# Making the second copy of a small weight on chip, in a fused attention and ReGLU kernel: one load instead of two, a matmul and two casts, the last tile's outputs in fresh buffers, and a new order of pieces

## The chip, the cores and the metric

The kernel runs on one core of one Trainium2 chip. The metric is the device time of an execution in microseconds (us), lower is better. Before the change, four runs gave 385.4, 385.94, 387.39 and 387.7 us; their median is 386.66. The engines are named as in the profile: PE (TensorE, matmul; PEld is its weight load), DVE (VectorE), ACT (ScalarE), POOL (GpSimd), SP (SyncE, which here only issues DMAs).

## What is computed

A linear attention with an exponential feature map, and a ReGLU feed-forward on its output. Shapes: q, k, v are 8 x 8 x 576 x 64 (batch, head, position, width), w_phi is 64 x 128, the feed-forward (FFN) has 4608 rows, width 512 and hidden width 1536; all in float32.

```python
def phi(x):
    proj = np.einsum('bhsd,df->bhsf', x, w_phi)
    proj = proj - np.max(np.abs(proj), axis=-1, keepdims=True)
    return np.concatenate([np.exp(proj), np.exp(-proj)], axis=-1)
q_p, k_p = (phi(q), phi(k))
kv = np.einsum('bhsf,bhsd->bhfd', k_p, v)
z = np.sum(k_p, axis=2)
num = np.einsum('bhsf,bhfd->bhsd', q_p, kv)
den = np.einsum('bhsf,bhf->bhs', q_p, z)[..., None] + 1e-06
x = num / den          # then rows (batch, position), columns (head, width)
gate = np.maximum(x @ w_gate, 0.0)
out = (gate * (x @ w_val)) @ w_out
```

## The kernel before

**Tiling.** Of the 576 positions of a batch, 512 are worked in four chunks of 128 rows; the last 64 ("tails") of two batches are put together into mixed tiles. Matmuls are bf16 with PSUM sums in float32. PSUM is one tile `pall` of eight banks of 512 float32 columns, and each piece of work is told by hand which banks it uses.

**Attention.** For each batch and each pair of heads (an item, u = 0 to 3) PE transposes k (L239; from batch 2 on a DMA does it), DVE copies the transpose to SBUF (L242), `rows_group` multiplies by w (L265) into a pair of banks, DVE takes the row maximum of the absolute values (L246), ACT makes exp of plus and minus the projection into `kp` (L279) and from the maximum the scales `ek` (L291, for batch 0 also a column of `vs`, L295), POOL scales v into `vs` (L250) and PE multiplies `kp` with `vs` into kv (L332, and L340 for the tail, whose scaled v is `vsm`); ACT copies kv (L348). For the first tail the scales are `ekm` (L302). For q, `q_rows` makes the projection twice, once as columns (L366, w as the weights) and once as rows for the maximum; ACT makes exp (L381 or L383/L384), PE multiplies with kv (`q_num`, L411: first 7 heads, then 1), DVE adds two terms into `u` (L420, L423) and takes the reciprocal `r` (L426), POOL divides into `xu` (L428), and `q_finish` transposes into `xT`: on PE with a DVE copy for batches 0 and 1 (L438, L444), by DMA on SP's queue after that (L434).

The projections contract over 64 rows only, so two heads lie in the two halves of the partitions, and w is needed in both halves: the tile `w2` is 128 x 128, w above w. It was made by two loads of w_phi into the two halves of `wf` on ACT's DMA queue (L1027) and one cast by ACT (L1037).

**FFN.** Nine groups: one for each batch's 512 rows and one for all the tails. In a group `half_step` makes twelve steps of x @ w_val (cast to `val_sb` by ACT, L475) and of x @ w_gate (DVE multiplies, L479) on PE (L466), and `out_step` multiplies with w_out in three parts (L492), after which ACT copies the tile to `out_sb` (L502) and SP stores it (L505; in the last group `store_pair`, L512, on SP's and ACT's queues). `out_last` (L519) makes the fourth tile of the last group in three column ranges of 256, 128 and 128, each copied by DVE (L528) and stored at once. `out_sb` has two buffers.

**What sets the order.** All of this is cut into 855 pieces, and the string `ORDER` says in which order the pieces are emitted, so it sets the order on every engine and queue at once. A token such as `44:0` is piece 44 with bank 0 (a pair starts at its first bank); `z22:0` is `keep_busy`, 22 units of 128 columns of a matmul on zeros (L1004) that computes nothing. Pieces 0 to 42 are the loads in the order of `LOADS`, 43 to 49 are the first item of batch 0 (transpose, projection, maximum with scales, two exps, vs, kv), 50, 57 and 64 begin the other three, 71 the first tail, 76 and 90 q of batch 0; 531 is the first FFN matmul. The first loads stand ahead of the list (L1022 to L1032).

The framework gives each DMA that SP or ACT issues one of eight completion lanes in turn; a DMA whose lane is still taken waits at the head of its queue for the DMA that held it. In the program's list of waits the second load of v's first tail (SP, L180) waits for the lane of the first V load.

Of the kernel before, what the change touches and what calls it, by code (L numbers as in the profile page):

```python
# [8 lines left out]
FP32 = mybir.dt.float32  # L9
BF16 = mybir.dt.bfloat16  # L10
# [36 lines left out]
ORDER = """z22:0 43:01 z1:2 50:2 44:0 0 z6:3 51:6 45 46 z5:5 64:5 47 57:4 71:3 48 z3:2 65:4 3 54 72:2 58:0 73  # L47
74 4 66 75 52 53 68 59 55 67 69 62 49:2 7 z16:3 76:3 60 56:6 8 1 61 2 90:7 77:42 91:60 78 79 9 70:2
5 93 63:3 108:4 103:5 120:0 83 94:13 92 6 95 96 z2:5 80:50 11 104:6 81:3 10 106 z20:4 100:45 84:02
101:5 85 82:4 105 12 114:5 531:4 86 102:0 532:1 87:76 115:4 109:2 126:0 117 537:1 547:6 110 13 17  # L50
88:7 111 538:0 97:16 553:7 545:0 107 116 539:6 121:2 127:0 112 129 122 546:7 16 14 123 89:4 132:5
540:6 98:7 533:4 145:5 549:6 128 554:7 176 124 133:24 118 135 130 534:6 134 15 550:7 136:04 137 138
113:2 99:3 125:6 174 548:7 555:5 119:6 146:30 131:2 148 19 543:7 139:62 551:0 140:1 541:7 142:26 147
542:0 158 177 143:1 535:7 552:6 168 195 544:2 149:03 169:6 556 20 150 151 170 171 141:2 557 21 144:3
155:40 536:1 558:2 559 189 190:3 560 191 18 152:01 561:7 159 175 183 193 153:2 564:6 156:5 565 192
160:02 161 201 196:4 162 227 566 562 197 198 154:2 157:3 163:01 563 164:62 22 214 571:3 199 172 229
583:1 567:0 184:2 178:4 186 179 568:1 579:0 180 185 584:7 573:6 200:1 580:0 202:24 181 204 247 23
203 182:7 589:6 194:1 572:0 187 25 205:42 248:6 26 206 188:1 575:0 207 249 241 574:2 228 250 576:3
211:45 587:0 173 235 208:12 577:3 212:0 569:7 242:5 230:2 295 232 243 244 590:4 24 570:7 209:1 297
578:0 585:4 581:7 231 215:50 217 586:4 588:7 210 216 582:2 218:03 236:5 245 251 213 219 29 237 597:7  # L60
233 591:2 598 220 239 224:01 238 225:3 592 221:41 279 599 310 252:0 226 253 222:3 593 240:5 266 223
254:60 256 246:4 296 304 234:5 289 255 280 594:3 33 335 165:2 257:04 258 259 30 595 600:2 166:7
290:4 291 596 27 263:67 292 601 602 167 298 264:7 260:30 261:1 603:6 28 615:7 617:0 316 294 267:24
311:6 313 293 269 268 604:1 312 262 607:0 616:4 31 348 618:5 605:1 606:6 305:2 270:40 265 271 609:7
623:6 272 306 356 608:0 308 307 624:1 276:45 273:07 625:6 613:1 626:5 614:2 36 281:36 317:0 282 35
314 611:5 322 619:2 400 283 318 32 621:6 277:7 620:3 284:24 612:5 319 274:3 309:7 315:6 610:4 299:0
320 323:25 278 301 325 275 622:7 350 627:4 362 324 285:56 628 34 629 300 630:7 302 326:25 357:0 42
327 328 636:4 358 631 321:5 632 401 416 351:2 352 637 349 360 353 633:5 634 635 37 639:6 354 303:7
638 647:2 286:3 359 329:56 368 640:7 655:4 330:6 332:23 657:5 287:7 418 649:4 658:6 331 336:02 363:4
361:7 643:6 338 364 39 644:7 425 437 650:2 656:3 38 648:6 333:7 334 337 365 641:2 651:3 339:06 369:4  # L70
340 341 659:2 645:3 370 355:6 342:70 374 660:1 652:2 646:3 402:60 371 419 438:4 469 366 403 404
642:2 367:3 653:0 372 431 439 343:1 405:26 373:7 440 654:3 345:70 661:1 346:6 662:2 672:5 673 344
410 432:3 375:06 434 441 376 663:2 347 674 433 377 664 665 435 669:3 378:04 411:6 379 387 670 412
666:2 380 667 384:01 381:45 413 417 414 668 671 382:1 675:0 385:2 471 687:7 388:53 420:0 390 421
691:2 422 676:7 692:3 679:4 689:7 693:2 389 40 690:3 680:4 383 688:7 288 677:0 391:13 392 386 393
426:5 697:7 427 698:0 41 521 443 415 442:3 394:41 428 694:2 423 397:73 483 683:0 398:1 681:4 395:2
695:5 424:6 678:0 696:7 484:5 444:31 429 436:0 446 445 485 477 682:7 685:0 430:1 684:2 699:7 486
686:3 705:4 478:5 447:02 480 700 449 448 706 489 470 479 456 399 396 707 708:2 701 453:35 709 450:46
711:7 702:5 451:3 454:6 710 703 457:03 704 717:2 459 481 458 712:7 723:6 718:5 719:7 460:30 461 487
472:5 508 462 725:2 473 726:7 731:0 466:13 732:4 729:2 724:7 452 463:01 730:4 475 522 464:7 467:3  # L80
455 713:2 474 715:1 714:0 495 727:4 716:7 490:5 496:20 498 720:4 497 465 468 721:7 491 744:0 492
738:1 406:74 722:2 728:3 733:4 734:2 488:3 745 407:7 482:6 746 735:2 493 499:35 494:7 500 741:0 501
476:7 739 740 502:34 742 505:15 743 753:6 506:7 736 737 503:3 747:4 509:05 749:7 510 748:2 754:3
767:4 755:7 511 751:3 504 752:2 512:04 514 750:3 756:2 523:64 513 768:3 759:2 525 760:0 757:1 515:23
516:0 758:4 518:51 765:3 524 766:2 763:0 780:1 519:3 764:4 761:5 769:0 507 762:2 770:7 777:0 526:65
774:7 517 778 771:2 520 527:34 775 528:5 776 779 772 785:3 408:0 787:4 795:5 529:3 781 782 773 783:0
784:1 786:7 796:0 788:6 791:7 793:5 789:6 803:7 792:0 790:1 804:2 797:0 805:1 813:7 798:0 794:6
810:5 801:4 799:6 800:3 814 802:4 409 806:6 811 530 816:0 812 815 807:6 819:1 808 817 831:7 809 818
823:7 820:1 827:0 828:2 825:1 824:0 821:7 826:6 841:5 822:7 832:6 829:0 833:7 839:1 840:0 830:2
842:1 835:0 836:7 834:6 837:5 846:7 838:6 843:0 847 848 852:1 853:2 854:3 844 849:7 845 850 851"""  # L90
# [6 lines left out]
def kernel(  # L97
# [56 lines left out]
    def psum_pair():  # L154
        i = plan.banks.pop(0)
        return pall[:, i : i + 2]
# [101 lines left out]

    def rows_group(halves, n=4):

        banks = psum_pair()
        for j in range(n):
            for i, (par, T4) in enumerate(halves):
                rows = slice(D * par, D * (par + 1))
                nc.tensor.matmul(  # L265
                    banks[:, i, F * j : F * (j + 1)], lhsT=T4[rows, j, :], rhs=w2[rows]
                )
        return banks[:, :, 0 : F * n].rearrange("p i (j f) -> p i j f", f=F)
# [188 lines left out]
    def ffn_pieces(g):  # L457
# [30 lines left out]
        def out_step(t, part):  # L488
            if part == 0:
                st["po", t] = psum()  # L490
            for fi in range(4 * part, 4 * part + 4):
                nc.tensor.matmul(  # L492
                    st["po", t],
                    lhsT=st["h2"][:, fi, P * t : P * t + P],
                    rhs=wo_sb[:, fi, :],
                    start=(fi == 0),
                    stop=(fi == NFC - 1),
                )
            if part < 2:
                return  # L500
            out_sb = sb_g.tile([P, DM], FP32, name="out_sb", bufs=2)
            nc.scalar.copy(out_sb, st["po", t])  # L502
            if g < B:
                rows = out[S * g : S * g + SF, :].rearrange("(p c) n -> c p n", c=C)
                nc.sync.dma_start(out=rows[t], in_=out_sb)  # L505
            else:
                store_pair(t, out_sb, 0, DM)

# [7 lines left out]
        def out_last(t, lo, hi):  # L516
            ps = psum()[:, 0 : hi - lo]
            for fi in range(NFC):
                nc.tensor.matmul(  # L519
                    ps,  # L520
                    lhsT=st["h2"][:, fi, P * t : P * t + P],
                    rhs=wo_sb[:, fi, lo:hi],
                    start=(fi == 0),
                    stop=(fi == NFC - 1),
                )
            if "last" not in st:
                st["last"] = sb_g.tile([P, DM], FP32, name="out_sb", bufs=2)
            nc.vector.tensor_copy(st["last"][:, lo:hi], ps)  # L528
            store_pair(t, st["last"], lo, hi)
# [8 lines left out]
        for n, (fis, lo, hi) in enumerate(steps):  # L538
            for name, w in (("wv", wv_sb), ("wg", wg_sb)):
# [13 lines left out]
                    (["h2"] if n == 0 else []) if gate else ["val"],  # L553
# [6 lines left out]
        for t in range(3 if g == B else 4):  # L560
            for part in range(3):
                ops = [("PE", NF * (0.0025 + DM / 2400))]
                if part == 2:
# [13 lines left out]
                    ["osb"] if part == 2 else [],  # L577
                    [("osb", 3), ("h2", 0, uses, g)] if part == 2 else [],
# [4 lines left out]
        if g == B:  # L583
            for i, (lo, hi) in enumerate(((0, 256), (256, 384), (384, 512))):
# [13 lines left out]
                    ["osb"] if i == 0 else [],  # L598
                    [("h2", 0, uses, g)] + ([("osb", 4)] if i == 2 else []),
                    [(g, "out", 3, i - 1)] if i else [],  # L600
# [386 lines left out]
    wf = singles.tile([P, F], FP32)  # L987
# [36 lines left out]
    )  # L1024
    for u in range(2):
        load_kqv(0, "kn", k, nc.sync, FP32, slice(2 * u, 2 * u + 2))
        nc.scalar.dma_start(out=wf[D * u : D * (u + 1)], in_=w_phi)  # L1027
# [5 lines left out]
    make_identity(nc, ident[FP32])  # L1033
    nc.gpsimd.tensor_copy(ident[BF16], ident[FP32])
    held = singles.tile([P, 1], FP32)
    nc.gpsimd.tensor_copy(held, inputs["kn", 0][:, 2, 0, 0:1])
    nc.scalar.copy(w2, wf)  # L1037
# [115 lines left out]
```

## Time and profile before

| | |
|---|---|
| median of 4 runs | 386.66 us (385.4 to 387.7) |
| the profiled execution's own time | 385.4 us |
| its span, first to last instruction | 383.6 us |
| idle PE up to the first FFN matmul at 31.08 | 8.7 us |
| after the last matmul (ends 379.1) to the end of the span | 4.5 us |

The page's section 2 cuts the span into 40 slices of 9.6 us; a digit is a busy share in tenths, PEclk the granted PE clock:

```profile
PE   7589999999999999999999999999999999999995
DVE  4479968767977788377957675487257643321430
ACT  3988857798868877759786967557555423224311
POOL 3776954476783565744267140623020201000000
PEclk9699999999999999999999999999999999999998
DMA  8979999989979998999157910301030112002004
```

PE is busy nearly throughout from the fourth slice on; the other engines thin out as the attention ends and only FFN is left. In the second slice the PE clock was low. A line of the timeline gives start, length, engine, line, operation, output and inputs, count, and in brackets the idle time just before with what ended it; the shares of the chain and the waits are inferred from semaphores, and the ends of matmuls are modelled.

### The profile page before, as it was taken

The numbers are of one execution on the slowest core, as the hardware profiler recorded it, in microseconds if no ns is written. First come the engines' busy times: TensorE is split into PE (matmuls) and PEld (weight loads), VectorE is DVE, ScalarE is ACT, GpSimd is POOL, SyncE is SP. The second block draws the span as 40 slices with busy tenths as digits, with TensorE's granted clock in tenths as the row PEclk, the third lists the DMA queues.
The fourth block names the chain that finished last, engine by engine and source line by source line (L and its number), as shares of the span: only waits on it lengthen the run. The fifth ranks groups of instructions, "written<-read, shape, count | busy, mean of one in ns | idle before, by whom it ended". The sixth has DMA issues, their size and how long they took to land.

```text
span 383.6 us, 8885 instructions
## 1 busy us (share of the span) xinstructions
PE 367.2 (96%) x3544; PEld 207.9 (54%) x3594; DVE 238.3 (62%) x410; ACT 242.3 (63%) x489; POOL 151.7 (40%) x166
## 2 busy tenths in 40 slices
PE   7589999999999999999999999999999999999995
PEld 4368988556465455555544555454644454444452
DVE  4479968767977788377957675487257643321430
ACT  3988857798868877759786967557555423224311
POOL 3776954476783565744267140623020201000000
PEclk9699999999999999999999999999999999999998
DMA  8979999989979998999157910301030112002004
GB/s 216 240 125 206 199 191 180 187 232 137 153 133 125 241 219 106 206 214 159 32 119 185 153 29 28 110 3 27 29 109 3 29 55 84 0 34 77 0 4 109
DMA packets 92282, 44.95 MB, mean 117 GB/s; under 512 B 58064, under 2 KB 87760, under 8 KB 92240
## 3 DMA queue, kind: packets, MB, share of 16 engines
q1 hardware_dynamic: 63328, 30.03, 35.9%
q0 software_dynamic: 28272, 13.77, 29.7%
q10 hardware_dynamic: 640, 0.59, 0.6%
q8 instruction: 28, 0.46, 0.5%
q14 instruction: 14, 0.11, 0.1%
HBM read 37.81 MB, written 9.44 MB: 123 GB/s over the span
## 4 chain that ended last, share of the span: by engine, by line
PE 92%; DMA 3%; issue 2%; ACT 1%; DVE 1%; SPq 0%; POOL 0%; DVEq 0%; POOLq 0%
PE pall L466 49%; PE pall L492 24%; PE pall L411 5%; PE pall L332 4%; PE pall L265 4%; PE pall L366 3%; DMA vt<-in_v_dram 2%; DMA vn<-in_v_dram 1%; PE pall L340 1%; PE pall L519 1%; PE pall L239 1%; ACT qp L383 1%; ACT qp L384 0%; PE pall L1004 0%; PE pall L438 0%
## 5 line engine op out<-in xcount | busy, mean ns | idle before, releaser
L479 DVE SCALAR_TENSOR_TENSOR h<-pall,val_sb 128x512 bf16<-128x512 f32 x108 | 74.0, 688 | 64.4 <-PE pall L466 60.9
L492 PE MATMUL pall<-wo_sb,h 128*128 128x512 bf16 x401 | 97.2, 379 | 1.3 <-issue 0.3
L475 ACT CAST val_sb<-pall 128x512 bf16<-128x512 f32 x108 | 63.0, 594 | 53.8 <-PE pall L466 48.7
L466 PE MATMUL pall<-xT,wv_sb 128*128 128x512 bf16 (+1 forms) x520 | 93.2, 320 | 0.6 <-DVE xT L444 0.2
L466 PE MATMUL pall<-xT,wg_sb 128*128 128x512 bf16 (+1 forms) x507 | 91.7, 319 | 1.1 <-issue 0.3
L428 POOL TENSOR_TENSOR xu<-u,r 128x512 bf16<-128x512 f32 x36 | 37.3, 1040 | 127.5 <-DVE r L426 104.6
L279 ACT ACTIVATE kp<-pall 128x1024 bf16<-128x1024 f32 (+1 forms) x74 | 70.4, 1009 | 5.1 <-PE pall L265 5.1
L250 POOL TENSOR_TENSOR vs<-vn,ek 128x1024 bf16<-128x1024 f32 x32 | 60.8, 1903 | 31.0 <-ACT ek L291 29.4
L466 PEld LDWEIGHTS <-wg_sb 128*128 128x128 bf16 x576 | 46.7, 98 | 39.9
L466 PEld LDWEIGHTS <-wv_sb 128*128 128x128 bf16 x576 | 46.4, 98 | 39.1 <-issue 0.3
L492 PEld LDWEIGHTS <-h 128*128 128x128 bf16 x420 | 38.4, 98 | 40.9
L246 DVE TENSOR_REDUCE mq<-pall 128x8 f32<-128x1024 f32 x36 | 43.9, 1221 | 13.3 <-PE pall L265 10.5
L246 DVE TENSOR_REDUCE mk<-pall 128x8 f32<-128x1024 f32 (+1 forms) x37 | 43.7, 1189 | 10.3 <-PE pall L265 5.2
L420 DVE TENSOR_TENSOR t<-pall,cq 128x455 f32<-128x455 f32 (+3 forms) x80 | 33.6, 420 | 26.3 <-PE pall L411 26.2
L502 ACT COPY out_sb<-pall 128x512 f32<-128x512 f32 x35 | 20.6, 589 | 37.3 <-PE pall L492 35.7
L383 ACT ACTIVATE qp<-pall 128x512 bf16<-128x512 f32 x60 | 36.6, 610 | 4.5 <-PE pall L366 4.3
L423 DVE TENSOR_TENSOR u<-pall,t 128x455 f32<-128x455 f32 (+3 forms) x80 | 34.2, 428 | 6.6
L384 ACT ACTIVATE qp<-pall 128x512 bf16<-128x512 f32 x60 | 37.1, 618 | 0.0
L411 PEld LDWEIGHTS <-qp 128*128 128x128 bf16 x640 | 28.2, 98 | 13.4 <-issue 0.4
L411 PE MATMUL pall<-kv,qp 128*128 128x65 bf16 x640 | 31.0, 194 | 0.3 <-ACT qp L384 0.2
L332 PE MATMUL pall<-vs,kp 128*128 128x65 bf16 x512 | 21.4, 196 | 3.1 <-ACT kp L279 2.2
L332 PEld LDWEIGHTS <-kp 128*128 128x128 bf16 x512 | 19.3, 99 | 7.6 <-ACT kp L279 2.4
(72 smaller groups left out, 260.6 us busy)
## 6 DMA issues: line engine op xcount, KB each, us to landing
out_dram<-out_sb SPq DMA_DIRECT2D x32, 256.0 KB, 2.4
vn<-in_v_dram SPq DMA_DIRECT2D x7, 1024.0 KB, 7.2
qn<-in_q_dram POOLq DMA_DIRECT2D x8, 512.0 KB, 8.2
kn<-in_k_dram POOLq DMA_DIRECT2D x7, 512.0 KB, 7.7
wv_sb<-in_moe_w_val_dram POOLq DMA_DIRECT2D x3, 512.0 KB, 10.3
wg_sb<-in_moe_w_gate_dram POOLq DMA_DIRECT2D x3, 512.0 KB, 13.9
wo_sb<-in_moe_w_out_dram POOLq DMA_DIRECT2D x3, 512.0 KB, 14.4
vt<-in_v_dram SPq DMA_DIRECT2D x6, 128.0 KB, 5.4
```

The costliest lines, as they stand in the source:

```text
L246: nc.vector.tensor_reduce(m, banks, axis=AX.X, op=ALU.max, apply_absolute_value=True)
L250: nc.gpsimd.tensor_tensor(dst[:, :, :, 0:D], src[:, :, None, :].to_broadcast([P, *dst.shape[1:3], D]), ek[:, :, :, None].to_broadcast([P, ...
L279: nc.scalar.activation(kp[:, s], st["rows"], AF.Exp, scale=(1.0, -1.0)[s])
L332: nc.tensor.matmul(kv_ps[:, hh, s, :], lhsT=st["kp"][:, s, c % 2, 2 * hh + c // 2], rhs=st["vs"][:, 4 * hh + c, s, :], start=(hh == s == c ...
L383: nc.scalar.activation(x["qp"][:, s, a], cols[:, 0], AF.Exp, scale=sign)
L384: nc.scalar.activation(y["qp"][:, s, b], cols[:, 1], AF.Exp, scale=sign)
L411: nc.tensor.matmul(banks[s][:, i], lhsT=x["qp"][:, s, slot, P * blk : P * (blk + 1)], rhs=kvs[b, h // 2][:, h % 2, s, :],)
L428: nc.gpsimd.tensor_tensor(x["xu"], x["u"][:, :, 0:D], r.to_broadcast([P, 8, D]), op=ALU.mult)
L466: nc.tensor.matmul(ps[:, n * i : n * (i + 1)], lhsT=w[:, dc, P * fi : P * fi + P], rhs=xT[:, dc, lo:hi], start=(dc == 0), stop=(dc == NDC ...
L475: nc.scalar.copy(st["val", step], ps)
L479: nc.vector.scalar_tensor_tensor(st["h2"][:, fis[0] : fis[-1] + 1, lo:hi], ps.rearrange("p (a b) -> p a b", b=n), 0.0, st["val", step].rea ...
L492: nc.tensor.matmul(st["po", t], lhsT=st["h2"][:, fi, P * t : P * t + P], rhs=wo_sb[:, fi, :], start=(fi == 0), stop=(fi == NFC - 1),)
```

## The change

- w_phi is loaded once, as 64 x 128, ahead of the k loads in program order, and cast by ACT to bf16 (`w1`). POOL writes `twice`, two 64 x 64 identities side by side, from the float32 identity, ahead of the bf16 identity. In front of the first projection PE multiplies `twice` with `w1`, which gives w above w in bank 7, and ACT copies it to `w2`.
- In the last group all four output tiles go into a tile that takes the room of `vn0` (a v buffer) instead of the two `out_sb` buffers, and the three column ranges of the fourth tile have to come after the other three tiles. Before, they stood ahead of the last two of them.
- `ORDER` is another list throughout, with other banks. There are 98 units of zeros instead of 77. The first wv load (piece 1) comes right after the loads of k and v of batch 1.
- With one DMA fewer the lanes shift by one: the second load of v's first tail waits for the second k load.

```diff
-ORDER = """z22:0 43:01 z1:2 50:2 44:0 0 z6:3 51:6 45 46 z5:5 64:5 47 57:4 71:3 48 z3:2 65:4 3 54 72:2 58:0 73
-74 4 66 75 52 53 68 59 55 67 69 62 49:2 7 z16:3 76:3 60 56:6 8 1 61 2 90:7 77:42 91:60 78 79 9 70:2
-5 93 63:3 108:4 103:5 120:0 83 94:13 92 6 95 96 z2:5 80:50 11 104:6 81:3 10 106 z20:4 100:45 84:02
...
-842:1 835:0 836:7 834:6 837:5 846:7 838:6 843:0 847 848 852:1 853:2 854:3 844 849:7 845 850 851"""
+ORDER = """z22:0 43:01 z6:2 44:6 45 50:5 0 46 z23:4 51:0 47 64:2 53 57:3 71:4 z5:5 58:2 3 72:6 60 73 61 48 4 52
+8 65:4 74 66 67 1 75 49:6 7 69 59 62 55 z11:7 76:7 90:6 9 68 z9:2 77:24 54 2 78 70:7 79 63:6 z4:0
+91:04 56:2 93 114:3 103:7 5 120:6 80:24 6 81:5 z7:3 104:6 83 92 z9:3 94:30 106 95 105 96 108:2 82:5
...
+839:7 842:5 833:6 849:7 834:0 840:1 843:2 838:0 844 850 845 846:3 851 847 848 852:4 853:5 854:6"""
...
+    w_ready = []
+
+    def both_halves_of_w():
+
+        ps = pall[:, 7, 0:F]
+        nc.tensor.matmul(ps, lhsT=twice.rearrange("p a b -> p (a b)"), rhs=w1)
+        nc.scalar.copy(w2, ps)
+        w_ready.append(True)
+
     def rows_group(halves, n=4):
 
+        if not w_ready:
+            both_halves_of_w()
         banks = psum_pair()
...
-            out_sb = sb_g.tile([P, DM], FP32, name="out_sb", bufs=2)
+            out_sb = sb_g.tile([P, DM], FP32, name="out_sb", bufs=2) if g < B else final(t)
             nc.scalar.copy(out_sb, st["po", t])
...
+        def final(t):
+
+            if "final" not in st:
+                st["final"] = sb_in.tile([P, H, C, D], FP32, name="vn0")
+            return st["final"].rearrange("p h c d -> p (h c d)")[:, DM * t : DM * (t + 1)]
...
-            if "last" not in st:
-                st["last"] = sb_g.tile([P, DM], FP32, name="out_sb", bufs=2)
-            nc.vector.tensor_copy(st["last"][:, lo:hi], ps)
-            store_pair(t, st["last"], lo, hi)
+            out_sb = final(t)
+            nc.vector.tensor_copy(out_sb[:, lo:hi], ps)
+            store_pair(t, out_sb, lo, hi)
...
-                    [(g, "out", 3, i - 1)] if i else [],
+                    [(g, "out", 3, i - 1)] if i else [(g, "out", t, 2) for t in range(3)],
...
-    wf = singles.tile([P, F], FP32)
+    wf = singles.tile([D, F], FP32)
+    w1 = singles.tile([D, F], BF16)
...
+    nc.scalar.dma_start(out=wf, in_=w_phi)
     for u in range(2):
         load_kqv(0, "kn", k, nc.sync, FP32, slice(2 * u, 2 * u + 2))
-        nc.scalar.dma_start(out=wf[D * u : D * (u + 1)], in_=w_phi)
...
     make_identity(nc, ident[FP32])
+    twice = singles.tile([D, 2, D], BF16)
+    nc.gpsimd.tensor_copy(twice, ident[FP32][0:D, None, 0:D].to_broadcast([D, 2, D]))
     nc.gpsimd.tensor_copy(ident[BF16], ident[FP32])
...
-    nc.scalar.copy(w2, wf)
+    nc.scalar.copy(w1, wf)
```

## The prediction

> **What bounds the kernel now.** I read the page's busy shares first, then the busy time by stretch, cut where the trace changes its character, then the chain of waits of the first 35 us, then the timeline there and at the end.
>
> ```profile
> PE 367.2 (96%) x3544; PEld 207.9 (54%) x3594; DVE 238.3 (62%) x410; ACT 242.3 (63%) x489; POOL 151.7 (40%) x166
> ```
> ```profile
> 0.00:31.08 31.08, 22.42 (x259) 14.82 (x260) 18.12 (x38) 22.50 (x53) 20.10 (x26) 0.89 0.99 195
> 31.08:371.90 340.82, 337.62 (x3231) 188.71 (x3280) 219.19 (x370) 218.01 (x434) 131.61 (x141) 1.00 0.65 111
> 371.90:379.10 7.20, 7.15 (x57) 4.37 (x55) 1.01 (x3) 1.17 (x2) 0.00 (x0) 1.00 0.28 73
> 379.10:383.70 4.60, 0.00 (x0) 0.00 (x0) 0.00 (x0) 0.58 (x1) 0.00 (x0) 0.72 0.43 116
> ```
> Columns: stretch, length, then busy us (count) of PE, weight load, DVE, ACT, POOL, then granted PE clock, DMA share, GB/s. From 31.08, the first FFN matmul, to 371.90 PE idles 3.2 us in 341: that stage is PE's own work, the new order can't take more than 3.2 us from it, and it can add. The two ends are open: 8.7 us idle in the first 31 (several us of the busy time there are matmuls on zeros that hold the clock up), and 4.6 us after the last matmul.
>
> The chain through the head, and the rows that set it:
> ```profile
> 1.76 5.64 DMA vn<-in_v_dram
> 7.42 6.22 DMA vt<-in_v_dram
> 13.85 1.81 issue
> 15.66 0.26 POOL vsm L257
> ```
> ```profile
> 6.44 0.30 ACT L1037 CAST w<-wf 128x128 bf16<-128x128 f32 x1 [4.21 <-DMA wf<-in_w_phi_dram]
> 6.79 0.40 PE L265 MATMUL pall<-w,tT 64*128 64x128 bf16 x8 [1.05 <-ACT w L1037]
> 7.23 1.22 DVE L246 TENSOR_REDUCE mk<-pall 128x8 f32<-128x1024 f32 x1 [0.76 <-PE pall L265]
> ```
> ```profile
> 12.50:19.30 6.80, 4.40 (x41) 3.19 (x42) 1.94 (x3) 6.02 (x19) 5.49 (x4) 0.50 1.26 261
> ```
> The second half of v's tail is only issued when an earlier V load has landed (7.4), and POOL waits for it until 13.81. Everything else in the head waits for w: the first projection stands 1.05 us for ACT's cast, and the cast for the second of w's two loads. And PE runs at half clock from 12.5 to 19.3.
>
> **The change part by part.** All sums are against this execution: span 383.6, time 385.4, so 1.8 us lie around it; it is 1.26 us below the median of 386.66.
>
> *One load of w instead of two.* Both loads stand on ACT's queue, not Pool's as the title has it; Pool gains a 64x128 copy. The tile's rows give 2.8 us to landing for the first (issued 0.97, so 3.8) and 4.7 for the second (1.6, so 6.3). The one that stays is first in its queue: 3.8. New on the path: w1's cast (0.30 by L1037, ready 4.2, hidden: PE is at its first transposes until about 4.7), 6 units of zeros (22 took 2.53 us at the start, so 0.7; to 5.4), the doubling matmul (between 0.05, the mean of eight in the row above, and 0.31, the lone 128-wide one at 4.57; I take 0.1, since it follows other matmuls), and the copy to w2 from PSUM (between 0.30, the cast above, and 0.40, a 128x260 copy of L348; 0.3, being the size of the cast). With 0.1 of hand-offs the projection starts at 5.9, not 6.79: **0.9 us earlier**. Without an early landing (6.3) it would start at about 7.2, 0.4 later than now. Behind ACT's wait for PE stand only exponentials that need w2 anyway. Pool's extra copy (at most 0.29, its cast of 128x128) lies in Pool's 1.31 us wait before `held`: nothing; uncovered 0.3 on the transposes that need `ident`.
>
> *A lane moves.* The listed waits of SP show that with one DMA fewer the second v-tail load waits for the second K load (issued 1.26, 3.1 to landing, so 4.4), not for the V load that lands at 7.4. It issues at 5.6 and, right behind the first half (5.0 plus 6.9), lands about 12.1 instead of 13.64. A bound from below is no gain, if it is the DMA rate (busy share above 1 until 19) that sets it; from above 1.8, the earlier issue. I take 1.5: it joins a queue whose previous piece is down at 11.9.
>
> *The head in the new order*, laid out from the instruction lists with the durations of this trace (now in brackets). DVE's maximum ends 7.55, so ACT's `ek` starts 7.6 [8.48]. ACT then has `ek`,`vs` 0.42, four exponentials of 0.94 and `ekm` 0.8: `ekm` is ready at 12.6 [12.5], since one more exponential stands before it. So `vsm` starts 12.6 [13.81] and the last matmuls of the first kv at 14.9 [15.96]. Then 11 + 9 units of zeros, 16 transposes and two 512-wide matmuls, at half clock 0.107 per 128 columns as zeros cost there: 4.7, so the first q projection is there at 19.6 and its exponentials start [20.96]. Pool's three `vs` (1.9 each) end at 20.6 [21.4], the last kv is copied at 22.8, the first numerators run at 23.2 [25.39]. DVE has two maxima and three casts before them, so `t` at 24.35 [26.41], `r` at 26.25, `xu` at 26.3 [28.48]; a tail maximum, a q maximum and a cast now stand ahead of xT's copy: 28.6 [30.64]. The first FFN matmul at 29.25 [31.08]: **1.8 us earlier**. The list of pieces ahead of it is the same in both orders, so PE has no more real work left after it. The zeros grow from 77 to 98 units: 1.1 us at full clock, all ahead of that matmul and inside this layout, so not counted again. At full clock throughout the same layout ends 0.8 earlier.
>
> Here a rule speaks against the change. The trace shows half clock for 6.8 us after PE had stood from about 10 to 13.5 with one 0.40 us group in it. In the new order PE stands from about 11.3 (16 kv matmuls that need only the first `vs`) to 14.9. The Trainium skill (TensorE: Matmul & The Clock Gate, "HAM oscillation — how this bites in real kernels") says that a gap above some 3.4 us puts PE back to half rate, at windows that run freely. By the row, half clock until 19.3 as now: 1.8 us gained. By the rule, a gap of 3.6 that starts later can bring a later window, half rate until about 26: PE has some 4 us (at full rate) of work there, that doubles, about 2 us of it has room beside ACT and DVE, so the gain is gone. I take the row: the gap is no longer than the present one and zeros fill more of what lies ahead of it.
>
> *Loads moved.* Pool issues the first wv load at about 10.7 instead of 21.39, into a time in which the DMA engines go idle later on (share 0.04 at 20 to 22), and the other four from 20.6, 0.5 earlier, with one load less ahead. Now they land about 2.6 us apart from 27.2 on; each should come about 3 us earlier, and PE wants them 1.8 earlier: hidden. Pool's 0.8 of issuing ends before `vsm`: nothing.
>
> *Tail.* PE's work is the same. Now the last tile ends in an ACT copy of 0.58 and 64 KB stores (2.0 and 2.3 us to landing); then in DVE's 128-wide copy of 0.29 and a quarter of the bytes (1.9 and 2.1 for 32 KB). So **0.45 us earlier** (0.3 to 0.7). The fresh output buffer takes away waits that the trace doesn't show on the path: the copies there wait for PE. Nothing.
>
> *The order from 31 to 372.* Every engine's list is another one. Between at best 3.2 us less and a loss that one late transfer sets; I take no change, as the stretches now idle by 0.1 to 0.7 us in every 30 to 70, and the supply starts earlier too.
>
> Sum: 1.8 + 0.45 = 2.3, 383.1 for the profiled execution, **384.4** for the median.
>
> **The rivals.**
> *Head gain absorbed*: half clock lasts on into 19 to 26, or the first FFN matmuls meet late weights. For it: the rule, and a DMA share of 1.2 to 1.5 from 24 to 60. Against it: PE waited for no weights there, 28.87 busy of 28.92. Only the tail stays: 386.2.
> *A stall in the middle (the other side)*: SP's queue is strict in order, and the new order sets other stores and V loads ahead of the transposes that make xT. SP's own waits now show 62.5 us in 13 on `xu`, 4.8 each, none reaching PE. One such wait laid bare on PE costs 4.8 against 2.3 gained: 389.2. From 2.3 us exposed it cancels the gain, from 4.2 it is slower by 0.5%. Against it: PE's 99% now with the same kind of queue.
> *w doesn't come earlier*: the one load lands at 6.3 like the present second. The head loses 1.3 of its 1.8: 385.7.
>
> **How the numbers follow.** As laid out 0.50 (own range 382.6 to 385.4: full clock or a tail gain of 0.7, against half of the head gain); absorbed 0.25; stall 0.20; w late 0.05. A measurement of this kernel can tell about 0.5% from no change, 1.9 us, so faster means below 384.7 and slower above 388.6. The likeliest case lies mostly below 384.7: faster 0.42. Its upper part, absorbed, w late and small stalls: same 0.38. Slower 0.20. The range goes from 382.6 up to 389.0, just short of the stall's own price.
>
> **What would show it.** The first projection at about 5.9; `vsm` at 12.6; the first wv matmul near 29.2; granted clock 1.00 from about 19.3; idle PE from there to the last matmul about 3 us; from the last matmul to the span's end about 4.1. A first projection after 6.8 refutes the w part, a clock of 0.5 after 20 gives the first rival, PE rows in the middle that wait for xT over 2 us in all the second.

## The result, and the profile after

The changed kernel takes 385.88 us (median of 35 runs, 382.97 to 389.12), the kernel before 386.81 in the runs beside it (56 runs, 384.58 to 388.34). The ratio is 0.9972 [0.996, 0.9985] (the bracket is its 95% interval): faster by 0.28%, about 1 us (0.93 between the medians, 1.1 by the ratio). The forecast was 2.3 us. The direction and the wide range came true; less than half of the sum came. A ratio is not simply the quotient of two medians: it leaves out the few executions that lie over 1.5% above the fastest of their kernel, while a median in us given with an experiment below includes them.

The first profile of the changed kernel is an unlucky execution: it took 387.69 us (span 385.9), 1.8 above its own median, while the profiled execution of before lay 1.3 below its own. Side by side these two would say that the change costs 2.3 us. So both kernels were profiled again, and readings below use four profiles.

The busy time by stretch, cut at the first FFN matmul and at the last matmul (stretch, length, then busy us and count of PE, weight load, DVE, ACT, POOL, then granted PE clock, DMA share, GB/s). Changed kernel, first profile:

```profile
0.00:32.71 32.71, 23.85 (x266) 14.82 (x267) 17.94 (x36) 21.65 (x55) 18.41 (x24) 0.90 1.06 201
32.71:382.27 349.56, 345.36 (x3290) 193.34 (x3338) 219.33 (x374) 220.24 (x436) 133.94 (x143) 1.00 0.62 109
382.27:385.90 3.63, 0.01 (x1) 0.00 (x0) 0.29 (x1) 0.00 (x0) 0.00 (x0) 0.82 0.31 86
```

Changed kernel, second profile (384.58 us):

```profile
0.00:31.14 31.14, 24.36 (x267) 15.11 (x267) 17.94 (x36) 21.88 (x55) 18.52 (x24) 0.95 1.08 206
31.14:379.17 348.03, 348.03 (x3338) 193.26 (x3338) 219.23 (x374) 220.42 (x436) 134.06 (x143) 1.00 0.63 110
379.17:382.80 3.63, 0.00 (x1) 0.00 (x0) 0.29 (x1) 0.00 (x0) 0.00 (x0) 0.87 0.31 85
```

Kernel before, second profile (387.71 us):

```profile
0.00:33.37 33.37, 23.91 (x259) 15.71 (x260) 18.30 (x38) 22.87 (x53) 20.09 (x26) 0.85 0.96 185
33.37:381.39 348.02, 348.02 (x3336) 193.03 (x3335) 220.08 (x373) 219.17 (x436) 131.58 (x141) 1.00 0.62 110
381.39:385.90 4.51, 0.00 (x0) 0.00 (x0) 0.00 (x0) 0.58 (x1) 0.00 (x0) 0.82 0.43 118
```

Read by rows: the tail is 3.63 against 4.51 in every profile, 0.9 gained. The middle, from the first FFN matmul to the last matmul, is 348.0 in both orders (before's first profile: 379.10 less 31.08, 348.02) except in the changed kernel's first profile, 1.5 longer; more profiles of the new order show the same further down. The head ends at 31.08 and 33.37 before, at 32.71 and 31.14 after: no gain that stands out of its own scatter. The better profiles of each kernel, 383.6 and 382.8 us of span, differ by 0.8, which is the tail.

The w part did what it says. The changed kernel's timeline, first profile (start, length, engine, line, operation, and in brackets the idle time before):

```profile
5.78 0.27 ACT L265 CAST w<-pall 128x128 bf16<-128x128 f32 x1 [1.62 <-PE pall L264]
6.10 0.40 PE L276 MATMUL pall<-w,tT 64*128 64x128 bf16 x8 [0.35 <-ACT w L265]
```

The first projection starts at 6.10 (5.95 in the second profile), against 6.79 and 8.35 before. But the chain of waits of the same profile goes through v's tail again:

```profile
5.67 9.24 DMA vt<-in_v_dram
...
15.12 1.81 issue
16.92 0.26 POOL vsm L257
```

The second half of v's tail is issued at 5.67, as foretold, and takes 9.24 us to land: 14.9, where 12.1 had been forecast and 13.64 was the landing before. PE's waits between 4 and 34 us (engine, tile, line, what it waited for: us in total, times, longest) in the changed kernel:

```profile
PE pall L343 <- ACT kp L290: 3.9, 1, 3.9
PE pall L351 <- POOL vsm L257: 1.6, 1, 1.6
PE pall L449 <- POOL xu L439: 1.3, 1, 1.3
```

and in the second profile of before, the wait for w first:

```profile
PE pall L265 <- ACT w L1037: 2.7, 1, 2.7
PE pall L332 <- ACT kp L279: 2.4, 1, 2.4
PE pall L340 <- POOL vsm L257: 1.4, 1, 1.4
```

PE's wait for w (2.7) is gone and the one for `kp`, ahead of the first kv matmuls, is 1.5 longer. That longer wait comes from the new order and not from the earlier w: the old order with w made on chip (the first experiment below) has

```profile
PE pall L343 <- ACT kp L290: 2.4, 1, 2.4
```

and all seven profiles of the old order have 2.1 to 2.4, whether w is early or late; the new order has 3.8 to 3.9, and 2.9 in the one kernel below that was built to shorten it.

### The profile page after: what moved, and what is told of

Read it like the earlier page. It is cut to its first block, busy times and chain, and to the rows that moved or that the text cites. A ratio compares the mean times of both kernels' runs of the same rounds, so it can differ in the third digit from the quotient of the medians.

```text
span 385.9 us, 8907 instructions
## 1 busy us (share of the span) xinstructions
PE 369.2 (96%) x3554; PEld 208.2 (54%) x3602; DVE 237.6 (62%) x410; ACT 241.9 (63%) x490; POOL 152.4 (39%) x167
## 4 chain that ended last, share of the span: by engine, by line
PE 91%; DMA 2%; ACT 2%; issue 2%; SPq 1%; POOL 0%; DVE 0%; POOLq 0%
PE pall L477 47%; PE pall L503 23%; PE pall L422 5%; PE pall L276 4%; PE pall L343 4%; PE pall L377 3%; DMA vt<-in_v_dram 2%; PE pall L351 1%; ACT qp L395 1%; PE pall L239 1%; PE pall L536 1%; SPq L163 1%; PE pall L1021 1%; ACT qp L394 1%; SPq L180 1%
## 5 line engine op out<-in xcount | busy, mean ns | idle before, releaser
L477 PE MATMUL pall<-xT,wg_sb 128*128 128x512 bf16 (+1 forms) x516 | 93.3, 320 | 1.8 <-issue 1.2
L422 PEld LDWEIGHTS <-qp 128*128 128x128 bf16 x640 | 28.2, 98 | 12.4 <-ACT qp L395 0.2
L513 ACT COPY out_sb<-pall 128x512 f32<-128x512 f32 x32 | 18.6, 591 | 21.2 <-PE pall L503 12.8
```

Source lines behind the costliest of these rows:

```text
L422: nc.tensor.matmul(banks[s][:, i], lhsT=x["qp"][:, s, slot, P * blk : P * (blk + 1)], rhs=kvs[b, h // 2][:, h % 2, s, :],)
L477: nc.tensor.matmul(ps[:, n * i : n * (i + 1)], lhsT=w[:, dc, P * fi : P * fi + P], rhs=xT[:, dc, lo:hi], start=(dc == 0), stop=(dc == NDC ...
```

## The experiments

Every kernel here computes the whole reference. Marks in the text are: the first projection, the start of `vsm`, the first FFN matmul, and the end (last matmul to the end of the span), each from that kernel's profile. PE "stands" where it is idle and waits; "half clock" is a granted clock of 0.5. Before's marks are 6.79, 13.81, 31.08, 4.51 and, in its second profile, 8.35, 15.42, 33.37, 4.51.

### Each part alone

**The w part alone**, in the old order:

```diff
+    nc.scalar.dma_start(out=wf, in_=w_phi)
     for u in range(2):
         load_kqv(0, "kn", k, nc.sync, FP32, slice(2 * u, 2 * u + 2))
-        nc.scalar.dma_start(out=wf[D * u : D * (u + 1)], in_=w_phi)
...
+        if not w_ready:
+            both_halves_of_w()
```

> The kernel before with w doubled on chip, its own order and tail. Theory A (the w part pays by itself, what the forecast expected of the head is lost behind it): the first projection at 6.2 to 6.3 instead of 6.79, 0.3 to 0.6 us faster than before, 386.3. Theory B (the w part's gain is covered by ACT and POOL anyway): first projection just as early, time within 0.2 us of before. Theory C (the shifted lane makes the tail of v later, DMA rate being the limit): vsm later than 13.8 and the time up to 1 us longer.

Measured: 386.0 us, 0.9999 [0.9976, 1.0021]. Marks 6.41, 13.53, 31.25, 4.52. The projection is earlier, the end of the head isn't: alone, w is worth nothing that these runs can tell from zero (the medians differ by 0.5 us, which the interval covers).

**The tail alone**, the old order with the columns last and `final(t)`:

```diff
-... 852:1 853:2 854:3 844 849:7 845 850 851"""
+... 844 849:7 845 850 851 852:1 853:2 854:3"""
...
+            out_sb = final(t)
```

> The kernel before with the last tile's columns last and fresh output buffers, nothing else. From the last matmul to the end of the span 3.6 us as in the profile after, instead of 4.5: 0.9 us faster than before by theory A, which holds that the whole measured gain of about 1 us is in w and tail. If the order pays (theory D), the tail gives 0.4 or less, as the forecast had it.

Measured: 385.9 us, 0.9976 [0.9955, 0.9998], 0.9 us. End 3.59; head as in before's second profile (8.21, 15.87, 33.88). This alone is nearly all of the change's gain.

**The new order with w loaded twice**, the changed kernel without the w part:

```diff
-    nc.scalar.dma_start(out=wf, in_=w_phi)
...
+        nc.scalar.dma_start(out=wf[D * u : D * (u + 1)], in_=w_phi)
...
-    nc.scalar.copy(w1, wf)
+    nc.scalar.copy(w2, wf)
```

> The changed kernel with w loaded twice as before: the new order and the tail stay. Theory A: the first projection comes at about 6.9 to 7.2, and the time is 0.6 to 1 us above the changed kernel, so about equal to before (386.6). If the w part is covered (theory B): equal to the changed kernel, 385.9.

Measured: 388.18 us, 1.0051 [1.0028, 1.0073]. Marks 7.07, 14.67, 32.99, 3.6. Set against the old order with the same tail (0.9976), the new order costs 0.75% when w is late. Its longest waits of PE:

```profile
PE pall L341 <- ACT kp L288: 3.8, 1, 3.8
PE pall L274 <- ACT w L1051: 1.9, 1, 1.9
```

Where the 0.75% goes isn't shown. The new order puts the first projection (piece 44) ahead of the second item's transposes (50), so PE runs out of work sooner (at 5.19, against 5.89 in the profile of the tail alone), but w landed earlier here, so the wait for w is no longer than there (1.9 against 2.3) and the first FFN matmul no later (32.99 against 33.88). What this profile has more of is half clock: from 8.2 to 11.6, 15.0 to 21.8 and 32.1 to 35.5 us, the last inside the middle, which is 1.1 us longer. The new order needs the w part. It doesn't follow that it gains by it.

**The two kernels once more**, unchanged, for their scatter:

> The changed kernel unchanged, for a second profile beside the others of this call and its time on the same chip. Of the 25 to 36 us marks: if the first profile was an ordinary draw, the first projection is at about 6.1, vsm near 15 and the first FFN matmul at 31 to 33, the tail 3.6, and 348.0 to 348.3 lie between first FFN matmul and last matmul. Time 0.2 to 0.4% below before.

> The kernel before, for a second profile. If the first was a lucky draw (it was 1.3 us under the median), this one has w's second load landing later than 6.3, so the first projection later than 6.79, up to the 8.2 of the tail-only profile, vsm at 14 to 16 and the first FFN matmul at 31.5 to 33.5; 348.0 from there to the last matmul and 4.5 after it, as ever.

Measured: the changed kernel 385.64 us, 0.9966 [0.9943, 0.9989], marks 5.95, 13.90, 31.14, 3.63; before 387.71 in its one execution. The head of one and the same program moves by 1.6 to 2.3 us from profile to profile.

### The clock

**A hold on zeros in PE's gap.** In the changed kernel PE stands from 11.07 to 15.01. 56 units of zeros were put ahead of piece 49 (`y56`; a helper `hold` issues them, two units to a matmul):

```diff
-8 65:4 74 66 67 1 75 49:6 7 69 ...
+8 65:4 74 66 67 1 75 y56:7 49:6 7 69 ...
```

> The changed kernel with 56 more units of zeros ahead of the first kv matmuls, in the upper half of bank 7, where PE stands for 3.9 us (11.1 to 15.0) in the profile. They fill 3.0 us at full clock. Clock theory: the half clock of 6.8 us that follows at 15.8 does not come, the first FFN matmul moves from 32.9 to about 30 or 31, and the time falls by 1 to 2 us against the changed kernel (384 to 385), with less spread between runs. Supply theory (v's tail by DMA, then POOL, sets the head): clock at 1.00 but the first FFN matmul stays within 0.5 us, time equal or, where zeros run into the kv matmuls, up to 0.5 us longer.

Measured: 389.06 us, 1.0069 [1.0044, 1.0095]. A miss, as an experiment: its timeline has the zeros behind the gap, not in it, since they too waited for `kp`.

```profile
16.09 4.88 PE L1034 MATMUL pall<-zeros 128*128 128x256 bf16 x28 [3.79 <-ACT kp L292]
```

It shows only that work put behind that gap is on the path: 4.88 us of zeros made it 3 to 4 us slower.

**Fewer zeros**, without three runs of zeros (24 units) that stand between q's pieces:

```diff
-8 65:4 74 66 67 1 75 49:6 7 69 59 62 55 z11:7 76:7 90:6 9 68 z9:2 77:24 54 2 78 70:7 79 63:6 z4:0
+8 65:4 74 66 67 1 75 49:6 7 69 59 62 55 76:7 90:6 9 68 77:24 54 2 78 70:7 79 63:6
```

> The changed kernel without the 24 units of zeros behind the first kv matmuls (11, 9 and 4 of them). Theory Z (the zeros run at half clock there and stand on PE's path, 0.107 each): the first q exps start 1.5 to 2.1 us earlier after the last kv-tail matmul than the 5.2 us of the profile after, the first FFN matmul 1 to 2 us earlier in runs with half clock, time 1 us or so below the changed kernel (about 384.8) with less spread. Theory S (supply: POOL's three vs products end at 22.7 and set the last kv, whatever PE does before): the first FFN matmul moves by less than 0.3, time equal. Theory H (the zeros hold the clock up): more half clock later, up to 1 us slower.

Measured: 385.81 us, 0.9956 [0.9924, 0.9987]. Marks 6.12, 14.68, 29.97, 3.67. The profile's first FFN matmul is 1.2 us earlier than in the better profile after, but the ratio is the same within the intervals (0.9956 against 0.9966 and 0.9972): its spans scatter more (standard deviation 1.9 us against 1.0 and 1.3, the executions that a ratio leaves out left out here too) and its mean clock is lower (0.989 against 0.992). That zeros taken out are paid back in clock in other executions is a reading of these two figures; the run doesn't settle it.

### v's tail

**The tail's loads ahead of V heads 4 to 7.** If the DMA rate sets the landing, not the issue, then moving the small needed loads ahead of a 512 KB one must bring the landing forward:

```diff
-    load_v(0, 4, 8)
     load_tail(inputs["vt", 0][:, 0:1], 0, 1, v, nc.sync)
+    load_v(0, 4, 8)
```

> The changed kernel with v's first tail loaded ahead of heads 4 to 7 of v. Theory S (the tail's landing at 14.9 sets vsm, and POOL's chain the head): vsm starts at 12.7, where ekm is ready, instead of 15.07; the first FFN matmul comes 1.5 to 2 us earlier; time 384 to 384.5. Theory Z (PE's zeros at half clock set it): vsm just as early, but the first FFN matmul gains less than 0.7.

Measured: 384.53 us, 0.9946 [0.9916, 0.9977]. Marks 5.76, 12.81, 30.02, 3.59. `vsm` stands where the prediction wanted it (12.6), and waits for the scales:

```profile
12.81 1.90 POOL L250 TENSOR_TENSOR vsm<-vt,ekm 128x1024 bf16<-128x1024 f32 x1 [0.72 <-ACT ekm L313]
```

**The same without the 24 zeros:**

> Both edits: no 24 units of zeros, and v's tail ahead of heads 4 to 7. If zeros and supply each set the path in part, this gains more than either alone: 2.5 to 3.5 us below the changed kernel, 382.5 to 383.5, faster than both kernels. If one of them is all, it equals that one.

Measured: 384.63 us, 0.9963 [0.9933, 0.9992]. Marks 5.66, 12.60, 28.49, 3.68. Again an earlier profile and no better median than with the early tail alone.

### Old order or new

Three kernels in the old order, put together from the edits above: w and tail; w, tail and the early v tail; tail and the early v tail with w loaded twice.

> The kernel before with w made on chip and with the new tail, in the old order otherwise. If the new order adds nothing by itself, this is as fast as the changed kernel: 0.2 to 0.4% below before (385.3 to 386). If w pays only in the new order, it equals the tail alone (0.24% below). If the new order costs time, it is faster than the changed kernel by over 0.2%.

Measured: 385.35 us, 0.9963 [0.9945, 0.9981]. Marks 6.30, 13.89, 31.82, 3.65. This is the change without its new order, and it is as fast as the change (0.9972 and 0.9966).

> The same with v's first tail loaded ahead of heads 4 to 7 of v. Supply theory: vsm at 12.6 instead of 13.5 to 15, first FFN matmul about 1 us earlier than with the old loads, 384.5 to 385. If the old order's wait of the first kv (for the tail's exps, 13.5) and the half clock set the head, no gain against the kernel without this edit.

Measured: 383.49 us (6 runs), 0.9901 [0.9872, 0.993]: the fastest of all, 3.4 us below before, with an interval that lies clear of the changed kernel's. Marks 6.28, 12.05, 29.96, 3.60. Its chain of waits through the head, where the landing of v's tail at 11.3 is no longer the last input of `vsm` (the scales are, at 12.0):

```profile
5.14 6.20 DMA vt<-in_v_dram
...
12.05 1.89 POOL vsm L250
13.94 0.22 POOL vsm L257
```

> The kernel before with the new tail and v's tail loaded early, w still loaded twice; beside the one that also makes w on chip (0.990 of before) this tells what w is worth once v's tail is there in time. Cover theory: with v's tail early nothing covers w any more, the first projection at 6.8 to 8.4 sets the head, and this is 0.3 to 0.6% slower than the kernel with w on chip (0.993 to 0.996 of before). If w is worth nothing even then: 0.990.

Measured: 385.2 us, 0.996 [0.9943, 0.9976]. Marks 7.48, 13.39, 30.69, 3.58. Its projection waits for the second w load:

```profile
7.48 0.40 PE L265 MATMUL pall<-w,tT 64*128 64x128 bf16 x8 [1.59 <-ACT w L1042]
```

Old order with the new tail, as ratios to before:

| | v's tail as it was | v's tail early |
|---|---|---|
| w loaded twice | 0.9976 | 0.9960 |
| w made on chip | 0.9963 | 0.9901 |

w is worth 0.13% in the left column, inside the intervals, and 0.6% in the right one, where they don't overlap; v's tail is worth 0.16% in the upper row, inside the intervals, and 0.6% in the lower one, where they don't overlap. The two inputs cover each other.

### Why the new order gains less from it

With all three edits the new order stands at 0.9946 and the old at 0.9901; the intervals overlap. Two ideas were tried on the new order with the early v tail.

**PE's stand made shorter**: the tail's exponentials (piece 74) one piece earlier on ACT.

```diff
-... 72:6 60 73 61 48 4 52
-8 65:4 74 66 67 ...
+... 72:6 60 73 74 61 48 4 52
+8 65:4 66 67 ...
```

> The changed kernel with the early tail of v and, on ACT, the tail's exps one piece earlier, so that the bank which the first kv needs is free at about 13.6 instead of 14.9: PE stands 2.5 us instead of 3.8. Clock theory: a stand of 2.5 us is too short for the half clock, which comes in fewer runs: mean clock up, spread down, 383.5 to 384 (0.5 to 0.8 us under the kernel with the early tail alone). If the half clock comes all the same and vsm sets the rest, no change within 0.3 us; the one exp of the third item that comes 1 us later may cost up to 0.5.

Measured: 385.2 us, 0.9937 [0.9909, 0.9964]. Marks 6.13, 12.80, 29.48, 3.66. PE's stand went from 3.8 to 2.9 us and the first FFN matmul came 0.5 us earlier, but the half clock came all the same, twice, and the second time it lay in the middle, which is 1.4 us longer:

```profile
29.20:32.70 3.50, 3.50 (x39) 2.97 (x37) 3.00 (x6) 2.43 (x4) 2.19 (x3) 0.51 1.24 207
15.58:19.00 3.42, 3.42 (x23) 2.23 (x22) 1.66 (x3) 3.20 (x8) 3.42 (x3) 0.50 1.20 249
```

**Fewer early zeros**: `z23` becomes `z4`, in case zeros delay real work.

```diff
-... 44:6 45 50:5 0 46 z23:4 51:0 ...
+... 44:6 45 50:5 0 46 z4:4 51:0 ...
```

> The changed kernel with v's tail early and with 4 instead of 23 units of zeros ahead of the second projection. Theory of the zeros in the way: in runs whose PE is still at half clock there, 23 units take 2.6 us (1.4 at full clock) and put the second projection at 9.9 instead of 8.4; with 4 it is at 8.3 to 8.6 in every run, spread down, and the time 0.2 to 0.4% under the kernel with the early tail alone (0.9946 of before), near the old order's 0.990. If they hold the clock: mean clock below 0.993 and no gain.

Measured: 385.88 us, 0.9979 [0.9951, 1.0007]. Marks 5.35, 12.81, 29.72, 3.59. No gain; the mean clock fell to 0.988 from 0.993. In the profile the second projection came at 7.67 instead of 8.07 and the first FFN matmul 0.3 earlier, and two gaps of PE in the middle (last section) took 2.4 us. Fewer early zeros don't help.

What makes the new order profit less isn't settled, but the profiles show two things. The first is the bank. In both lists the first kv (piece 49) takes the bank of the first tail's projection (72), which is free when the tail's exponentials (74) are done. In the new list other exponentials stand before those on ACT. So, with all three edits, PE starts the first kv in the new order at

```profile
15.04 1.04 PE L343 MATMUL pall<-vs,kp 128*128 128x65 bf16 x16 [3.79 <-ACT kp L290]
15.88 0.41 PE L351 MATMUL pall<-vsm,kp 128*128 128x130 bf16 x2
```

and in the old one at

```profile
12.98 1.06 PE L343 MATMUL pall<-vs,kp 128*128 128x65 bf16 x16 [2.23 <-ACT kp L290]
14.20 0.38 PE L351 MATMUL pall<-vsm,kp 128*128 128x130 bf16 x2 [0.15 <-POOL vsm L257]
```

The run with piece 74 moved confirms the bank: the last two of these matmuls then started at 14.95. The second is the middle. It is 348.0 us in all seven profiles of the old order, and 1.1 to 2.8 us longer in five of the nine of the new one: three have gaps of PE, and three (one of them with a gap too) have a stretch of half clock that starts between 29 and 34 us and reaches past the first FFN matmul. How often that happens in executions without a profile isn't known.

## Where the prediction failed, and where it held

**The step that failed: "A lane moves"**, in the prediction's words "lands about 12.1 instead of 13.64 ... I take 1.5". The issue did move, from 7.42 to 5.67. The landing didn't. Set side by side, issue plus time to land:

| kernel | issued | to land | landed |
|---|---|---|---|
| before, two profiles | 7.42, 9.01 | 6.22, 6.24 | 13.64, 15.25 |
| changed, two profiles | 5.67, 5.7 | 9.24, 7.8 | 14.91, 13.5 |
| changed, fewer zeros; with the hold | 5.7, 5.9 | 8.9, 10.0 | 14.6, 15.9 |
| old order with w; with w and tail | 5.7, 5.67 | 7.7, 8.05 | 13.4, 13.72 |
| old order, v's tail ahead; with w too | 5.14, 5.14 | 7.27, 6.20 | 12.41, 11.34 |
| changed, v's tail ahead | 5.1 | 5.4 | 10.5 |

Issued up to 1.75 us earlier than in before's first profile, it takes 1.5 to 3.8 longer. It stands behind V heads 4 to 7 in DMA engines that are full (in the changed kernel's first profile the share is 1.11 from 5 to 12 us and 1.37 from 12 to 16.5), and only a place ahead of that load brought the landing forward, as it must if the rate sets the landing and not the issue. Whether the first wv load, which the new order issues at about 11 us into the same engines, adds to the later landings of that order no run separates. The prediction had named this as its lower bound, "no gain, if it is the DMA rate that sets it", with the share above 1 in hand, and took the end nearer to the other side; its reason, that it joins a queue whose previous piece lands at 11.9, put that piece's landing down as free of the same rate: it landed at 13.7 and 12.4. Where v's tail was early and w made on chip, `vsm` started at 12.05 (old order) and 12.81 (new) against 12.6, and the first FFN matmul came at 29.96 and 30.02: 1.1 of the 1.8 us, counted from before's first profile. In time this is shown for the old order (0.9901 against 0.9963); in the new one the intervals overlap (0.9946 against 0.9972).

A second term of the prediction's layout was put at nothing: the bank. The layout has PE stand from 11.3, behind "16 kv matmuls that need only the first `vs`". They needed their bank too, and ran after the stand, at 15.01 and 16.13 in the changed kernel. So even with `vsm` at 12.81 the last matmuls of the first kv started at 15.88 and not at 14.9.

Six profiles have w on chip and v's tail as it was. In three (the changed kernel's first and the two of the old order) the landing set the last matmuls of the first kv. In the other three PE had stood for `kp` until 16.1 to 16.3 and lost nothing to `vsm` after it. In the changed kernel's second profile, one of these, the scales `ekm` were as late as v's tail, at 13.81: the 23 units of zeros ahead of the second item's transposes took 2.59 us there and 1.41 in the first profile:

```profile
7.39 2.59 PE L1021 MATMUL pall<-zeros 128*128 128x512 bf16 x6
```

That is 0.113 us a unit, the pace of the 22 units at the start (2.52 us), though the profile grants PE 1.00 in that stretch: by this pace the slow start of PE ended about 4 us later in one execution than in the other.

**w: right, and more than forecast, but covered.** The single load landed 2.9 us after its issue (2.8 taken). The second load of the pair took 4.7 to land in before's first profile and 6.3 in its second, 6.1, 5.4 and 5.0 in three other kernels, so w saves more than the 0.9 that one profile showed. Of the bounded costs, the doubling matmul took 0.28, near the upper end of its range (0.1 taken), and the copy 0.27, and the projection came at 6.10 and 5.95 in the changed kernel, for 5.9 forecast (5.35 to 6.41 over all kernels with w on chip). None of it reached the end that the runs can show: alone 0.9999, on the new tail 0.13%.

One effect of the late w stands in no sum of the prediction. In four of the five profiles with w loaded twice PE stood 1.6 to 2.7 us for it, and in each of these four a stretch of half clock followed, from 8.2 to 9.4 us on. In before's second profile:

```profile
8.70:12.10 3.40, 3.40 (x25) 1.89 (x23) 2.25 (x4) 2.06 (x6) 1.66 (x1) 0.52 1.32 238
```

The fifth, before's first, stood 1.05 us and has none there. In the eleven profiles with w on chip PE stands 0.4 us for it, and no half clock starts before 12 us. What this is worth in time isn't separated.

**The tail: right, a term mis-sized.** 0.45 forecast, 0.9 measured, outside 0.3 to 0.7. The last stores of before had been taken as 64 KB. They are 128 KB, as the DMA issues of the last microseconds say (size and median us from issue to landing), before:

```profile
out_dram<-out_sb SPq DMA_DIRECT2D x1, 128.0 KB, 2.3
out_dram<-out_sb ACTq DMA_DIRECT2D x1, 128.0 KB, 2.8
```

and after, for the stores that now come last:

```profile
out_dram<-vn SPq DMA_DIRECT2D x2, 32.0 KB, 1.8
out_dram<-vn ACTq DMA_DIRECT2D x2, 32.0 KB, 2.0
```

So the landing shrinks by 0.8 on the slower queue and the copy by 0.29 (0.58 to 0.29): 1.1 by the rows, 0.9 by the marks.

**The clock: the window floats, as the rule has it; the row didn't hold, and the rule's threshold didn't either.** The prediction took half clock to 19.3 as before, and weighed against it the rule of the Trainium skill (TensorE: Matmul & The Clock Gate, "HAM oscillation — how this bites in real kernels") that a gap above some 3.4 us puts PE back to half rate; that the windows run freely stands on the same page under "What's actually happening". PE stood 11.07 to 15.01 (11.3 to 14.9 forecast), and then, in the changed kernel's first profile:

```profile
15.83:22.65 6.82, 5.43 (x31) 3.36 (x31) 1.38 (x2) 3.23 (x9) 6.82 (x6) 0.51 1.17 252
```

Half clock to 22.65; 16.6 to 20.0 in the second profile; 12.5 to 19.3 in before's first profile, 8.8 to 12.2 and 15.6 to 22.5 in its second. The window floats, 3.4 or 6.8 us long, and 19.3 was one draw. Half clock to 22.65 goes with a head that ends at 32.71, to 20.0 with 31.14. But the length of the gap doesn't decide here: no profile of the old order has a stand above 2.7 us, and each has half clock for 6.8 us or more in the head; the stands for w above and the one of 2.9 us are further cases. So the page's threshold doesn't hold in these profiles. Over 46 executions of the changed kernel the mean granted clock goes with the span: 382.7 us on average at 0.993 or more (20), 384.4 at 0.990 to 0.991 (17), 385.5 at 0.989 or less (9). In 105 executions of before the same three groups lie at most 0.7 us apart (384.5, 385.2 and 385.2). That the clock causes this scatter is argued from the correlation, not shown by a run.

**The first rival came close in time (386.2), not in cause.** A clock of 0.5 after 20 was named as its sign, and was seen. But in the second profile that clock was back at 20.0 and the head still ended at 31.14: `vsm` had started at 13.90, no earlier than before. What held `vsm` up, v's tail at 13.5 and the scales at 13.81, lies ahead of that stretch of half clock, so in that execution the later window isn't what took the head's gain.

**The middle: no change forecast, 0 and 1.5 us longer in the two profiles.** Up to 3.2 us of idle PE had been seen as the most to gain. That idle time isn't there: before's second profile has 348.02 busy in 348.02, and the first lacks some 50 matmul records (3286 against 3336). The rival of a stall that waits for xT didn't come; losses of another kind did, the gaps below and half clock past the first FFN matmul.

**The sum**: tail 0.45 forecast and 0.9 measured; head and middle together 1.8 forecast and about 0.2 measured (0.9972 against 0.9976 for the tail alone), inside the intervals. That the whole came to 1 us of 2.3 and not to less is owed to the tail's mis-sized term, which is luck. The old list has 75 units of zeros, not 77, so 23 were added; at the price taken that is 0.1 us.

## What to carry to other kernels

Before an input is made earlier, list every input of the join behind it: here w and v's tail each hid the other, and two edits worth 0.1 to 0.2% apart were worth 0.75% together. Where the DMA engines are full, as in this head, don't count an earlier issue as an earlier landing; put the small load that is needed ahead of the large one that isn't. When the order changes, ask of each piece also when its bank comes free. Take two profiles before adding up marks below a microsecond, and check the size of each store at the end, since the last one decides.

## What the hardware showed that was not expected

A single profile lay 1 to 2 us off the median of its own program: the second w load landed 4.7 or 6.3 us after its issue, half clock lasted 3.4 or 6.8 us, and PE's slow start ended early or late.

In three of nine profiles of the new order PE has gaps of 0.9 to 1.5 us between 53 and 66 us, four in all, inside a group of matmuls and with nothing that it waits for. The changed kernel's first profile:

```profile
64.94 0.73 PE L477 MATMUL pall<-xT,wg_sb 128*128 128x128 bf16 x10 [1.24 <-issue]
```

and the new order with the early v tail and fewer early zeros, which has two:

```profile
54.79 0.90 PE L477 MATMUL pall<-xT,wg_sb 128*128 128x128 bf16 x13 [0.90 <-issue]
...
63.45 0.45 PE L477 MATMUL pall<-xT,wg_sb 128*128 128x128 bf16 x5 [1.51 <-issue]
```

None of the seven profiles of the old order has one. Each gap ended 2.3 to 3.0 us after a 16 KB packet began on the queue that brings instructions, at a DMA share of 1.3 to 1.7; but such a packet comes every 4 to 12 us there, and most are followed by no gap. That PE's instructions came late is an inference; no run took the loads away there. In the changed kernel's first profile the gap makes 1.24 of the middle's extra 1.5 us.
